# Attention and a gated FFN on one core: two head pairs in five bursts, pair nine turned on TensorE, and the first weight columns asked for earlier

## The chip, the cores and the metric

The kernel runs on one core of a Trainium2 chip. The metric is the device time of one execution in microseconds (us); lower is better. A core has TensorE (PE, matmuls, with its weight loads shown as PEld), VectorE (DVE), ScalarE (ACT), GpSimd (POOL) and SyncE (SP, which here only issues DMAs). SP, ACT and POOL issue the transfers that 16 DMA engines carry out.

## The reference, cut to what matters

Attention with 4 sink positions and a window of 128, on q, k and v of shape (4, 8, 768, 64), followed by a feed-forward layer with a ReLU gate on the 3072 tokens that result:

```python
scores = scale * np.matmul(q, k.transpose(0, 1, 3, 2))
keep = is_sink | in_window                 # rel >= 0 and rel < 128, or pos < 4
scores = np.where(keep, scores, -1000000000.0)
a = np.exp(scores - np.max(scores, axis=-1, keepdims=True))
a = a / (np.sum(a, axis=-1, keepdims=True) + 1e-09)
attn_out = np.matmul(a, v)
x = attn_out.transpose(0, 2, 1, 3).reshape(B * S, H * D)          # (3072, 512)
gate = np.maximum(x @ w_gate, 0.0)                                # w_gate (512, 1536)
out = (gate * (x @ w_val)) @ w_out                                # w_out (1536, 512)
```

Inputs and output are fp32; the matmuls run in bf16.

## The kernel before

The work is cut into 16 units, U[0] to U[15]: unit i is head pair i % 4 of batch i // 4. Pair nine is U[8], the first of batch 2. A unit passes through these steps:

- Loads (L105 to L120, issued on SP): k, q and v of the two heads go into one of four fp32 staging tiles. For a unit turned on PE (`xbar` false) k and q are read as contiguous rows of 1536 B; for one turned by DMA (`xbar` true, batches 2 and 3) in pieces of 256 B.
- Casts to bf16 (L122 to L130) on POOL; the first unit's k and q on DVE and ACT.
- Turning k and q so that the head dimension lies on the partitions: `T` (L140 to L156) is twelve PE transposes and two ACT copies, `X` (L132 to L136) is two DMA transposes on SP. `sinkk` (L158 to L162) then makes, on DVE, a copy of some key blocks with the four sink keys in front.
- `S(gi)` (L169 to L187), three groups: scores on PE for both heads at once (64 rows of the array each), the exponential on ACT, and a mask multiply on DVE. In batch 0 the mask is added on PE instead, by a matmul with `bias`.
- `V` and `norm` (L192 to L210, L268 to L280), two parts of 384 queries: on PE the sums (weights of ones) and the outputs (weights of v), each head in 64 columns of the array; on DVE a transpose, a reciprocal, a transpose and the multiply that writes xT, the FFN's input.

The FFN runs in 96 chunks (L285 to L298): 4 batches, 2 halves of 384 tokens and 12 blocks of 128 hidden columns. A chunk is four matmuls gp, a ReLU on ACT (gs), four matmuls vp, and on DVE the multiply hT = gs * vp. When a half is done, `ffn2` (L302 to L315) makes the output tiles, twelve matmuls op each, three of which are put behind each later chunk; ACT copies a finished tile and SP stores it.

The order is written out by hand and each engine keeps it. The attention work is a list of stages (L376 to L436): per unit [s(0), v, s(1), t, s(2), v0] for the first eight units, where v is part 1 of the unit before, t turns the next unit and v0 is part 0 of this one. For units 8 to 15 the six are joined to three: [v, s(0)], [t, s(1)], [v0, s(2)]. Stage t also issues the loads and casts of unit x+3, on SP and POOL, and the weights: each of four column quarters of w_gate and w_value is one DMA issued by POOL (L222 to L226), which converts to bf16 on the way. `PLAN` (L444) gives the number of stages that are to be emitted before chunk ci. In between, linearly:

```python
PLAN = ((0, 28), (24, 50), (48, 62), (71, 74))
```

So 28 stages (units 0 to 3 and the start of unit 4) run before chunk zero, and from chunk 24 on one stage comes every two chunks. I call what stands between two chunks a burst. PSUM pools: `ps_gv` (three buffers of one bank) holds gp and vp, and before chunk zero the sums and outputs of V and the transposes of k; `ps_at` (two buffers of two banks) holds scores and, from chunk zero on, the sums and outputs; `ps_op` (one) the op tile. The helper `held` (L343 to L347) sets a byte of the staging tile on DVE, so that the load behind it waits until DVE has come to that place.

Of the kernel before, what the change touches and what calls it, by code (L numbers as in the profile page):

```python
# [10 lines left out]
BF16 = mybir.dt.bfloat16  # L11
# [22 lines left out]
def kernel(  # L34
# [12 lines left out]
    nc = tc.nc  # L47
    B, H, S, D = q.shape
    assert (B, H, S, D) == (4, 8, 768, 64)
    NP = H // 2  # L50
    scale = 1.0 / (D ** 0.5)
    d_model, d_ff = moe_w_gate.shape
# [6 lines left out]
    xpool = ctx.enter_context(tc.tile_pool(name="xp", bufs=2))  # L59
# [18 lines left out]
    wg = const.tile([128, KO, d_ff], BF16, name="wg")  # L78
    wv = const.tile([128, KO, d_ff], BF16, name="wv")
# [10 lines left out]
    class Unit:  # L90
# [3 lines left out]
        def __init__(self, i):  # L94
            self.i, self.b, self.p, self.s = i, i // NP, i % NP, i % 2
            self.kn, self.qn, self.vn, self.stg = kn[i % 3], qn[i % 3], vn[i % 4], stg[i % 4]
            self.xbar = self.b>1
            self.biased = self.b == 0

        def staging(self, x):  # L100
# [118 lines left out]
            nc.tensor.matmul(out=warm_ps[0][:, 0:128], lhsT=ident[:], rhs=ident[:], start=True, stop=True,  # L219
                             skip_group_check=True)  # L220

    def load_w(c):  # L222
        n = d_ff // 4
        for w, dst in ((moe_w_gate, wg), (moe_w_val, wv)):
            nc.gpsimd.dma_start(out=dst[:, :, c * n:(c + 1) * n],  # L225
                                in_=w.rearrange("(ko ki) n -> ki ko n", ki=128)[:, :, c * n:(c + 1) * n])  # L226

    def load_wo(c):
        nc.gpsimd.dma_start(out=wo[:, 4 * c:4 * c + 4, :],
                            in_=moe_w_out.rearrange("(ko ki) n -> ki ko n", ki=128)[:, 4 * c:4 * c + 4, :])  # L230
# [12 lines left out]
    def setup_slot(s):  # L243
        nc.vector.memset(kT[s][:, S:872], 0.0)
# [20 lines left out]
    xTs = {}  # L265
    ready = {}

    def norm(u, part, pool=ps_at):  # L268

        c0, w, _ = PARTS[part]  # L270
        nb = w // 32
        o, sums = u.V(part, pool)
        r = rpool.tile([128, 2, 384], F32, name="R")
        rc = dpool.tile([128, 12], F32, name="rc")
        nc.vector.transpose(r[:, 0, 0:w], sums[:, 0:w])  # L275
        nc.vector.reciprocal(rc[:, 0:nb], r[:, 0, 0:w].rearrange("p (b j) -> p b j", j=32)[:, :, 0])
        a = rc[:, 0:nb]
        nc.vector.transpose(r[:, 1, 0:w], bass.AP(a.tensor, a.offset, [a.ap[0], [1, nb], [0, 32]]))  # L278
        ready[u.b, u.p] = c0 + w
        nc.vector.tensor_tensor(xTs[u.b][:, u.p, c0:c0 + w], o[:, 0:w], r[:, 1, 0:w], op=Alu.mult)  # L280
# [37 lines left out]
    with tc.manual_schedule():  # L318
        U = [Unit(i) for i in range(B * NP)]
        on_array = []  # L320

        def at(x):
            return U[x] if 0 <= x < len(U) else None

        def casts(u, what, eng=nc.gpsimd):
            for w in what:
                u.cast(w, eng)

        def load_t(b):

            nc.sync.dma_start(out=vt[b % 2][:], in_=v[b, :, 744:768, :].rearrange("h s d -> s h d"))  # L331

        def cast_t(b):
            nc.gpsimd.tensor_copy(v6[b % 2][0:24, :, :], vt[b % 2][:])

        def load(x):
            if not U[x].p:
                load_t(U[x].b)
            for f in (lambda e: U[x].load_kq("k", e), lambda e: U[x].load_kq("q", e),
                      lambda e: U[x].load_v(e, 0), lambda e: U[x].load_v(e, 1)):  # L340
                f(nc.sync)

        def held(x):  # L343

            if x < len(U):
                nc.vector.memset(U[x].stg[0:1, 0:1], 0.0)
                load(x)  # L347

        for y in ("k0", "q0", "k1", "q1", "v1", "t", "k2", "q2", "v2", "k3", "q3", "v3"):
            if y == "t":  # L350
                load_t(0)
            elif y[0] in "kq":
                U[int(y[1])].load_kq(y[0], nc.sync)
            else:
                for h in (0, 1) if y[0] == "v" else ("ab".index(y[0]),):
                    U[int(y[1])].load_v(nc.sync, h)
        nc.vector.memset(ones[:], 1.0)
        setup_pool()
        setup_m0()
        nc.scalar.activation(ee[0][:, 0, 0, 0:64], ones[:], Act.Exp, bias=0.0, scale=1.0)  # L360
        for h in range(2):
            U[0].load_v(nc.scalar, h)
        for x in range(2):
            nc.vector.memset(v6[x][:], 0.0)
        setup_slot(0)
        setup_slot(1)
        warm(36)
        casts(U[0], "k", nc.vector)
        casts(U[0], "q", nc.scalar)
        casts(U[1], "kq")  # L370
        casts(U[0], "v")
        cast_t(0)
        casts(U[1], "v")
        casts(U[2], "kqv")
        load(4)


        stages = []

        def unit_stages(x):  # L380
            u, prev, nxt = U[x], at(x - 1), at(x + 1)

            def s(gi):
                def f():
                    if gi == 0 and u.p == 0:
                        xTs[u.b] = xpool.tile([128, NP, S], BF16, name="xT")
                    if gi == 0 and nxt is not None and nxt.xbar:
                        nxt.X()
                    u.S(gi)
                    if x == 0 and gi < 2:  # L390
                        warm(5)
                return f

            def v():
                if prev is not None:
                    norm(prev, 1, ps_at if on_array else ps_gv)

            def t():
                if nxt is not None:
                    if not nxt.xbar:  # L400
                        nxt.T(not on_array)
                    nxt.sinkk()
                if x == 3:
                    load(6)
                elif x == 4:
                    load(7)
                elif x >= 5:
                    held(x + 3)
                if 4 <= x < 6:
                    for c in ((0,), (1, 2))[x - 4]:  # L410
                        load_wo(c)
                if at(x + 3) is not None:
                    casts(at(x + 3), "kqv")
                    if (x + 3) % NP == 0:
                        cast_t((x + 3) // NP)
                if x in (0, 1, 3, 4):
                    load_w((0, 1, 1, 2, 3)[x])
                if x == 0:
                    load(5)
            def v0():  # L420
                norm(u, 0, ps_at if on_array else ps_gv)

            def both(f, g):
                return lambda: (f(), g())
            if x < NP:
                return [s(0), v, s(1), t, s(2), v0]
            return [both(v, s(0)), both(t, s(1)), both(v0, s(2))] if x >= 8 else [s(0), v, s(1), t, s(2), v0]

        def first():
            U[0].T(True)  # L430
            U[0].sinkk()
            setup_m1()
        stages.append(first)
        for x in range(len(U)):
            stages += unit_stages(x)
        stages.append(lambda: norm(U[-1], 1))  # L436

        si = 0
        f2 = deque()
        total = len(stages)  # L440

        ORDER = [(0, h, m) for g in range(0, FM, 3) for h in range(2) for m in range(g, g + 3)]
        ORDER += [(b, h, m) for b in range(1, B) for h in range(2) for m in range(FM)]
        PLAN = ((0, 28), (24, 50), (48, 62), (71, 74))  # L444

        def want(ci):
            for (c0, w0), (c1, w1) in zip(PLAN, PLAN[1:]):
                if ci <= c1:
                    return w0 + (w1 - w0) * (ci - c0) // (c1 - c0)
            return total  # L450
        count = {}
        n = S // 2
        for ci, (b, h, m) in enumerate(ORDER):
            if b not in hTs:
                hTs[b] = hpool.tile([128, FM, S], BF16, name="hT", tag="hT")
            while si < min(total, want(ci)):
                stages[si]()
                si += 1
            if not ci:
                on_array.append(1)  # L460
            chunk(b, h * n, n, m)
            for _ in range(min(3, len(f2))):
                f2.popleft()()
            count[b, h] = count.get((b, h), 0) + 1
            if count[b, h] == FM:
                for t in range(3 * h, 3 * h + 3):
                    w = d_model // 2 if (b, t) == (B - 1, 5) else d_model
                    for c in range(0, d_model, w):
                        for mm in range(FM):
                            f2.append(lambda b=b, t=t, mm=mm, c=c, w=w: ffn2(b, t, mm, b == B - 1, c, w))  # L470
        while f2:
            f2.popleft()()
# [33 lines left out]
```

The softmax here doesn't subtract the row's maximum and nothing guards it: scores larger than these inputs give would overflow.

## Time and profile before

| what | value |
|---|---|
| median of 8 runs (lowest, highest) | 260.83 us (258.87, 262.15) |
| the profiled execution's own time | 262.15 us |
| its span in the profile | 260.3 us |
| PE busy | 248.5 us, 95% |
| DVE, ACT, POOL busy | 144.1, 115.8, 61.6 us |
| chunk matmuls gp and vp | 384 and 384, 78.5 and 78.1 us |
| output matmuls op | 70.6 us |
| mean granted PE clock | 0.998 |

Busy time of an engine counts instructions that overlap once. Matmuls overlap each other: the duration of one matmul is longer than its distance to the next, so PE work is read from the starts. A timeline line gives the start in the span, the time from the first start to the last end of the merged instructions, the engine, the line of code, the operation with what it writes and reads, how many there are, and in brackets the engine's idle time before it. A line of the waits gives who waited for whom, the total, how often, and the longest.

### The profile page before, as it was taken

The page shows a single profiled execution, that of the slowest core. Times are in us where ns is not written, and L with a number is a line of the kernel's source. Part 1 is how long each engine was busy: PE and PEld are TensorE (multiplying, and loading weights), DVE is VectorE, ACT ScalarE, POOL GpSimd, SP SyncE. Part 2 cuts the span into 40 slices and gives each one's busy share as a digit, 9 for nine tenths or more (in the row PEclk, how much of TensorE's full clock was granted, in tenths as well). Part 3 has the DMA queues.
Part 4 walks back from the last instruction along what each step waited for, and adds up shares of the span by engine and source line. Part 5 has one row for each costly group of instructions (what it writes and reads, how often), then busy time and mean ns, then how long its engine had stood idle before and what let it go on. Part 6 is the DMA issues. An engine that isn't in the chain of part 4 may idle for free.

```text
span 260.3 us, 5178 instructions
## 1 busy us (share of the span) xinstructions
PE 248.5 (95%) x2023; PEld 143.7 (55%) x2046; DVE 144.1 (55%) x313; ACT 115.8 (44%) x188; POOL 61.6 (24%) x94
## 2 busy tenths in 40 slices
PE   7899699999979999999999999999999999999994
PEld 7565355656545555555555555556555555555443
DVE  2498859786839574666666574756664322322100
ACT  2877753646524444354534444443533333333212
POOL 6679528901453320404030120000000000000000
PEclk9999999999999999999999999999999999999999
DMA  7999998999999956948792951311011001111132
GB/s 217 304 278 280 219 228 204 179 207 196 216 113 227 225 123 124 162 109 154 73 250 63 181 104 42 60 43 40 3 40 40 21 21 40 43 40 40 40 109 96
DMA packets 77320, 33.56 MB, mean 129 GB/s; under 512 B 64368, under 2 KB 74352, under 8 KB 77296
## 3 DMA queue, kind: packets, MB, share of 16 engines
q1 hardware_dynamic: 69920, 28.12, 48.6%
q0 software_dynamic: 5808, 4.72, 11.9%
q10 hardware_dynamic: 1568, 0.39, 0.7%
q8 instruction: 16, 0.26, 0.4%
q14 instruction: 8, 0.07, 0.1%
HBM read 28.51 MB, written 6.29 MB: 134 GB/s over the span
## 4 chain that ended last, share of the span: by engine, by line
PE 74%; DMA 12%; SPq 10%; POOL 1%; issue 1%; ACT 0%; DVE 0%; POOLq 0%; ACTq 0%; DVEq 0%
PE op L310 23%; PE gp L290 21%; PE vp L296 20%; PE ops L206 6%; DMA stg<-in_v_dram 6%; SPq L119 5%; DMA wv<-in_moe_w_val_dram 4%; PE sps L181 3%; SPq L114 2%; DMA kT<-kn 2%; SPq L111 1%; SPq L331 1%; POOL vn L129 1%; PE tkq L149 1%; POOL wg L225 0%
## 5 line engine op out<-in xcount | busy, mean ns | idle before, releaser
L298 DVE TENSOR_TENSOR hT<-gs,vp 128x384 bf16<-128x384 f32 x96 | 52.7, 550 | 55.5 <-PE vp L296 53.9
L290 PE MATMUL gp<-xT,wg 128*128 128x384 bf16 x384 | 78.5, 327 | 2.2 <-DVE hT L298 1.6
L296 PE MATMUL vp<-xT,wv 128*128 128x384 bf16 x384 | 78.1, 326 | 1.9 <-DMA wv<-in_moe_w_val_dram 1.9
L293 ACT ACTIVATE gs<-gp 128x384 f32<-128x384 f32 x96 | 47.1, 491 | 62.5 <-PE gp L290 61.3
L310 PE MATMUL op<-wo,hT 128*128 128x512 bf16 (+1 forms) x277 | 70.6, 370 | 1.2
L185 ACT ACTIVATE ee<-sps 128x1006 bf16<-128x1006 f32 (+2 forms) x48 | 46.1, 966 | 46.9 <-PE sps L181 46.8
L296 PEld LDWEIGHTS <-wv 128*128 128x128 bf16 x384 | 37.5, 98 | 27.0 <-DMA wv<-in_moe_w_val_dram 2.3
L290 PEld LDWEIGHTS <-wg 128*128 128x128 bf16 x384 | 34.0, 98 | 32.1 <-issue 6.1
L310 PEld LDWEIGHTS <-hT 128*128 128x128 bf16 x300 | 29.4, 98 | 25.0
L187 DVE TENSOR_TENSOR ee<-ee,msk 128x1006 bf16<-128x1006 bf16 (+2 forms) x36 | 25.1, 698 | 11.6 <-ACT ee L185 11.6
L126 POOL CAST kn<-stg 128x768 bf16<-128x768 f32 x15 | 13.1, 875 | 61.0 <-DMA stg<-in_k_dram 56.0
L314 ACT COPY ot<-op 128x512 f32<-128x512 f32 (+1 forms) x25 | 14.2, 569 | 24.5 <-PE op L310 22.5
L275 DVE STREAM_TRANSPOSE R<-ops 128x384 f32<-128x384 f32 x24 | 14.0, 582 | 12.7 <-PE ops L206 12.5
L278 DVE STREAM_TRANSPOSE R<-rc 128x384 f32<-128x384 f32 x32 | 18.5, 578 | 1.1
L280 DVE TENSOR_TENSOR xT<-ops,R 128x384 bf16<-128x384 f32 x32 | 17.8, 557 | 1.7
L206 PEld LDWEIGHTS <-ones 128*64 128x64 bf16 x288 | 12.3, 109 | 11.2 <-issue 10.8
L129 POOL CAST vn<-stg 128x768 bf16<-128x768 f32 x16 | 13.3, 830 | 14.8 <-PE gp L290 7.0
L126 POOL CAST qn<-stg 128x768 bf16<-128x768 f32 x15 | 13.0, 864 | 12.6 <-DMA stg<-in_q_dram 12.1
L206 PE MATMUL ops<-ee,vn 128*64 128x255 bf16 (+7 forms) x256 | 15.3, 240 | 0.2 <-DVE xT L280 0.2
L181 PE MATMUL sps<-qT,kT 64*128 64x251 bf16 (+2 forms) x128 | 14.7, 252 | 0.5 <-ACT qT L154 0.4
L181 PEld LDWEIGHTS <-kT 64*128 64x128 bf16 x128 | 6.3, 93 | 12.9 <-issue 10.9
L161 DVE COPY kTs<-kT 128x372 bf16<-128x372 bf16 x16 | 6.4, 399 | 11.0 <-ACT kT L154 6.9
(57 smaller groups left out, 141.1 us busy)
## 6 DMA issues: line engine op xcount, KB each, us to landing
stg<-in_k_dram SPq DMA_DIRECT2D x16, 384.0 KB, 4.7
stg<-in_q_dram SPq DMA_DIRECT2D x16, 384.0 KB, 5.3
out_dram<-ot SPq DMA_DIRECT2D x23, 256.0 KB, 2.0
stg<-in_v_dram SPq DMA_DIRECT2D x30, 192.0 KB, 5.3
wg<-in_moe_w_gate_dram POOLq DMA_DIRECT2D x4, 384.0 KB, 8.4
wv<-in_moe_w_val_dram POOLq DMA_DIRECT2D x4, 384.0 KB, 10.4
wo<-in_moe_w_out_dram POOLq DMA_DIRECT2D x3, 512.0 KB, 13.7
stg<-in_v_dram ACTq DMA_DIRECT2D x2, 192.0 KB, 7.7
```

The source lines that it names most:

```text
L126: cp((self.kn if what == "k" else self.qn)[:], self.staging(what).rearrange("p h (n d) -> p n h d", d=64))
L181: nc.tensor.matmul(out=ps[:, h, c:c + w], lhsT=self.kw(j, r), rhs=qT[s][r, qa:qa + w], start=not self.biased, stop=True, skip_group_check= ...
L185: nc.scalar.activation(x, ps[:, :, 0:c], Act.Exp, bias=0.0, scale=scale)
L187: nc.vector.tensor_tensor(x, x, bc(msk[:, m0:m0 + c], 2), op=Alu.mult)
L206: nc.tensor.matmul(out=ps[1 - what][64 * h:64 * h + 64, qa - q0:qa - q0 + w], lhsT=self.vw(j, h) if what else ones[:], rhs=ee[s][:, gi, h, ...
L278: nc.vector.transpose(r[:, 1, 0:w], bass.AP(a.tensor, a.offset, [a.ap[0], [1, nb], [0, 32]]))
L280: nc.vector.tensor_tensor(xTs[u.b][:, u.p, c0:c0 + w], o[:, 0:w], r[:, 1, 0:w], op=Alu.mult)
L290: nc.tensor.matmul(out=gp[:, 0:n], lhsT=wg[:, ko, m * 128:(m + 1) * 128], rhs=x[:, ko, c0:c0 + n], start=ko == 0, stop=ko == KO - 1)
L293: nc.scalar.activation(gs[:, 0:n], gp[:, 0:n], Act.Relu, bias=0.0, scale=1.0)
L296: nc.tensor.matmul(out=vp[:, 0:n], lhsT=wv[:, ko, m * 128:(m + 1) * 128], rhs=x[:, ko, c0:c0 + n], start=ko == 0, stop=ko == KO - 1)
L298: nc.vector.tensor_tensor(hT[:, m, c0:c0 + n], gs[:, 0:n], vp[:, 0:n], op=Alu.mult)
L310: nc.tensor.matmul(out=op, lhsT=hTs[b][:, m, t * 128:(t + 1) * 128], rhs=wo[:, m, c0:c0 + n], start=m == 0, stop=m == FM - 1)
```

## The change

Four things are edited.

1. `load_w` takes a range of 128-column thirds. The first 128 columns of the first quarter of w_gate and w_value are asked for on POOL between the casts of U[2]'s q and v, the other 256 between the casts of U[3]'s q and v. Before, the whole quarter was asked for behind U[3]'s casts.
2. `xbar` begins at unit 9 in place of unit 8: U[8] is turned on PE in stage t of U[7].
3. The first four units run s(0), s(1), v, t, s(2), v0.
4. From U[8] on two units u and w share five stages: scores (u,0) and (u,1); outputs of the unit before u, both parts (for U[7] part 1 alone), with the loads ahead and w's sink copy; scores (u,2) and (w,0); outputs of u, both parts; scores (w,1) and (w,2). The DMA transposes are issued with the first and third of them. There are 70 stages in place of 74, and `PLAN` has one more point.

The xT tile of a batch is allocated at its first use in `norm`, which adds no instruction. The diff, cut to its core:

```diff
-            self.xbar = self.b>1
+            self.xbar = i>8
...
-    def load_w(c):
-        n = d_ff // 4
-        for w, dst in ((moe_w_gate, wg), (moe_w_val, wv)):
-            nc.gpsimd.dma_start(out=dst[:, :, c * n:(c + 1) * n],
-                                in_=w.rearrange("(ko ki) n -> ki ko n", ki=128)[:, :, c * n:(c + 1) * n])
+    def load_w(c, which="gv", m=(0, 3)):
+        for x in which:
+            w, dst = (moe_w_gate, wg) if x == "g" else (moe_w_val, wv)
+            a, b = c * 384 + m[0] * 128, c * 384 + m[1] * 128
+            nc.gpsimd.dma_start(out=dst[:, :, a:b], in_=w.rearrange("(ko ki) n -> ki ko n", ki=128)[:, :, a:b])
...
-        casts(U[2], "kqv")
+        casts(U[2], "kq")
+        load_w(0, m=(0, 1))
+        casts(U[2], "v")
         load(4)
...
+        def ahead(x):
+            if x == 3:
+                load(6)
+            elif x == 4:
+                load(7)
+            elif x >= 5:
+                held(x + 3)
...
+            if x == 0:
+                casts(U[3], "k")
+                casts(U[3], "q")
+                load_w(0, "g", (1, 3))
+                load_w(0, "v", (1, 3))
+                casts(U[3], "v")
+            elif at(x + 3) is not None:
+                casts(at(x + 3), "kqv")
...
             if x < NP:
-                return [s(0), v, s(1), t, s(2), v0]
-            return [both(v, s(0)), both(t, s(1)), both(v0, s(2))] if x >= 8 else [s(0), v, s(1), t, s(2), v0]
+                return [s(0), s(1), v, t, s(2), v0]
+            return [s(0), v, s(1), t, s(2), v0]
+
+        def pair_stages(x):
+            u, w, nxt = U[x], U[x + 1], at(x + 2)
...
+            first_outs = outs(U[x - 1], 1) if x == 8 else outs(U[x - 1], 0, 1)
+            a = then(scores((u, 0), (u, 1)))
+            a_ = then(first_outs, lambda: ahead(x), w.sinkk)
+            c = then(scores((u, 2), (w, 0)))
+            d = then(outs(u, 0, 1), lambda: ahead(x + 1), lambda: nxt is not None and nxt.sinkk())
+            e = scores((w, 1), (w, 2))
+            first = [then(turn(w), a)] if w.xbar else [a, turn(w)]
+            second = [then(c, turn(nxt))] if nxt is None or nxt.xbar else [c, turn(nxt)]
+            return first + [a_] + second + [d, e]
...
-        for x in range(len(U)):
+        for x in range(8):
             stages += unit_stages(x)
-        stages.append(lambda: norm(U[-1], 1))
+        for x in range(8, len(U), 2):
+            stages += pair_stages(x)
+        stages.append(lambda: (norm(U[-1], 0), norm(U[-1], 1)))
...
-        PLAN = ((0, 28), (24, 50), (48, 62), (71, 74))
+        PLAN = ((0, 28), (6, 32), (24, 50), (48, 62), (71, 70))
```

## The prediction, as recorded before the run

> **What bounds the kernel now.** I first read the busy table in 40 slices, then the list of waits, then the timelines of TensorE (PE) and VectorE (DVE) around each PE gap. The slices show PE full except at the start, around slices 5 (33 us) and 11 (75 us), and at the end:
>
> ```profile
> PE   7899699999979999999999999999999999999994
> DMA  7999998999999956948792951311011001111132
> ```
>
> The span is 260.3 us, its execution took 262.15 us, the median is 260.83. So time can come only from the two holes or from PE work. The list of waits names the holes:
>
> ```profile
> DVE kTs L161 <- DMA kT<-kn: 4.1, 1, 4.1
> ...
> PE vp L296 <- DMA wv<-in_moe_w_val_dram: 1.9, 1, 1.9
> PE gp L290 <- DVE hT L298: 1.6, 1, 1.6
> ...
> PE gp L290 <- DMA wg<-in_moe_w_gate_dram: 0.6, 1, 0.6
> ```
>
> The first hole is 0.59 + 1.91 = 2.50 us: chunk zero waits for the first weights (issued at 21.62 and 22.49, landed 8.8 and 10.6 us later). The second is 1.58 us: DVE stands 4.06 us before the sink copy of pair nine (U[8]), whose kT comes from a DMA transpose issued late, and an hT multiply queued behind it holds a PSUM buffer that gp needs.
>
> What DVE did under the first hole matters too (start, duration):
>
> ```profile
> 29.17 0.56 DVE L280 TENSOR_TENSOR xT<-ops,R 128x384 bf16<-128x384 f32 x1
> 29.66 0.69 DVE L187 TENSOR_TENSOR ee<-ee,msk 128x1006 bf16<-128x1006 bf16 x1
> 30.27 0.58 DVE L275 STREAM_TRANSPOSE R<-sums 128x384 f32<-128x384 f32 x1
> ...
> 31.82 0.56 DVE L280 TENSOR_TENSOR xT<-ops,R 128x384 bf16<-128x384 f32 x1
> ```
>
> The xT that chunk zero reads is ready at 29.73; the next normalization ends at 32.38. It reads PSUM from the pool that gp and vp share.
>
> In the full stretch the bursts of attention between chunks are the only thing on PE that is not a dense stream:
>
> ```profile
> 93.46 0.81 PE L310 MATMUL op<-wo,hT 128*128 128x512 bf16 x3
> 94.20 0.53 PE L206 MATMUL ops<-ee,ones 128*64 128x119 bf16 x10
> 94.58 0.50 PE L206 MATMUL ops<-ee,vn 128*64 128x119 bf16 x8
> 94.92 0.18 PE L206 MATMUL ops<-ee,v 128*64 128x20 bf16 x2
> 95.03 0.28 PE L181 MATMUL sps<-qT,kT 64*128 64x255 bf16 x2
> 95.15 0.27 PE L181 MATMUL sps<-qT,kTs 64*128 64x248 bf16 x2
> 95.35 0.82 PE L290 MATMUL gp<-xT,wg 128*128 128x384 bf16 x4
> ...
> 98.82 0.59 PE L310 MATMUL op<-wo,hT 128*128 128x512 bf16 x2
> 99.35 0.28 PE L181 MATMUL sps<-qT,kT 64*128 64x251 bf16 x2
> 99.47 0.27 PE L181 MATMUL sps<-qT,kTs 64*128 64x248 bf16 x2
> 99.67 0.82 PE L290 MATMUL gp<-xT,wg 128*128 128x384 bf16 x4
> ```
>
> Read the starts. Three op matmuls take 0.65 (86.51 to 87.16, where gp follows); before a V they take 0.74, so entering V costs 0.09. Two take 0.43 (82.40 to 82.83), before an S 0.53: entering S costs 0.10. Inside V the sums take 0.38 and the equal columns of ops 0.45 until S starts: leaving V costs 0.07 (0.05 for the shorter part, 89.20, 89.53, 89.91). The first pair of S takes 0.12, the equal second one 0.20 until gp: leaving S costs 0.08.
>
> [...] V runs as 128*64, S as 64*128, the chunks as 128*128[...], and S to S or V to V would not switch. [...] with the weights in flight the v load issued at 28.95 took 12.0 us, those before 22 us mostly 5.3 to 7. [...] Pair nine's k and q come in 256 B pieces now; its q took 18.7 us, beside weights, so size and company aren't separated.
>
> **The change, part by part.**
>
> (1) Early first columns. POOL finishes the casts of U[2]'s k and q at 15.36 and then stands until 16.83 for v. The two new issues (0.75 each, as the other weight issues) fit there: free. The other two thirds go out at about 19.9, before U[3]'s v cast, which moves from 20.28 to about 21.5; its reader, V at 26.8, has 4 us left. The four issues replace two, and later POOL work stands where it stood. If the 8.8 to 10.6 us to landing hold, the first columns are there by 27 and the rest by 31.3: chunk zero no longer waits. What is late next is DVE. With E the end of the xT multiply (29.73), gp0 starts at E + 0.05; vp0 needs the buffer that the first transpose of the next normalization frees, E + 0.6 (mask) + 0.6; gp1 follows at E + 1.9; vp1 needs the end of that normalization (E + 2.65); the transposes of U[5] take 0.67 (46.59 to 47.26). So gp2 starts at E + 4.0. Before it was at 35.79 = E + 6.06. Gain 2.06, not 2.5. Cover: if the first columns come after 29.7, each us late costs one.
>
> (2) Scores one and two ahead of V in the first four pairs. Moving one S (0.85) before V gives DVE the kT copy earlier: its two waits of 0.47 and 0.50 for ACT's kT copy go, but DVE then waits about 0.3 twice for the later sums. Walking PE, ACT and DVE by these durations puts E 0.4 earlier. Against it stands the queue sharing: 0.5 MB of weights now travels while k and q of U[3] and U[4] do (q of U[3] landed 18.95, its cast ended 19.93, PE wanted it at 20.8). Bounds: gain 0.5 to loss 1.5. I take a gain of 0.2.
>
> (3) Pair nine on PE. Twelve transposes add 0.67 on PE; the two ACT copies (0.80 each) have room (ACT is busy 4 to 5 of 10 us there). SP loses two transposes and loads k and q in 1536 B runs. The 1.58 goes, with 0.1 before the S at 80.55. Net gain 1.0. Bounds: 1.68 is the most; a loss of 0.67 if the wait only moves to pair ten, the first on the DMA transpose now.
>
> (4) Five bursts for six. Before, two pairs made twice [V,S] [S] [V,S]: 4 x 0.09 + 4 x 0.06 + 2 x 0.10 + 6 x 0.08 = 1.28. After: [S,S] [V,V] [S,S] [V,V] [S,S]: 2 x 0.09 + 2 x 0.06 + 3 x (0.10 + 0.08) = 0.84. Saves 0.44, times four: 1.8. Bounds: 0.3 a group of two pairs less if S,S and V,V pay as apart (0.3 in all), 2.4 if every one of the six switches is worth 0.10. What [V,V] puts at risk: two normalizations (2.03 each), the staging memset and the sink copy (0.45) now stand ahead of hT on DVE. From the burst's start: V done 0.8, norms done 4.8, sink copy done 5.2. The next burst, whose second S reads kTs, is two chunks later at 1.55 + 3.9 = 5.45 and gets there at 5.75: 0.55 of slack. PSUM for vp two chunks on is wanted at 6.65, hT is done at 5.75. DMA transposes: issued a burst earlier, about 4 us to landing (80.93 to DVE's use at 84.97), used after some 8.7.
>
> (5) The new plan holds one stage back in the first chunks and is level at chunk 24. Weights must then come earlier: wv quarter three landed at 51.65, wanted at 55.69 - 2.3 - 0.7 = 52.7. Free with 1 us left. Allocating xT later costs nothing: no instruction.
>
> Sum: 2.06 + 0.2 + 1.0 + 1.8 = 5.1. On the execution of 262.15: 257.05. The median is 0.5% below that execution, so 5.1 x 0.995 = 5.0 off 260.83: **255.8**.
>
> **The rivals.** A: queue sharing. Loads of U[3] and U[4] land 1.5 later, PE waits at their transposes, (2) becomes a loss: 5.1 - 1.7 = 3.4, 257.4. For it: 12.0 against 5.3 us landing. Against: POOL waited for v, not for k and q, at 16 us. B: the DMA stall moves to pair ten: 3.5 left, 257.3. For: it is the next on that path, in small pieces. Against: its transposes at 80.93 caused no wait and pair nine's loads ahead of it now get lighter. C: merged bursts save nothing beyond 0.3: 257.2. D, slower: at each of the seven [V,V] bursts with a sink copy, DVE is late and holds PE. It decides from 5.1 / 7 = 0.73 of stall each, so with the sink copy ending at 6.5 instead of 5.2; at the 1.58 that pair nine's cost, 11.1 - 5.1 = 6 slower, 266.8. For: 1.58 shows that a late sink copy reaches PE. Against: DVE is busy 6 of 10 us there.
>
> **How the numbers follow.** 255.8 (its own range 254.6 to 256.9) has 0.58, A 0.13, B 0.09, C 0.07, D 0.07, more than I count (2.5 for (1), 2.4 for (4): 254.3) 0.06. Low 254.0 and high 258.5 leave out D and tails. A measurement of this kernel can tell about 0.5% (1.3 us) from no change: faster by more has A to C and most of the rest, 0.87; same 0.05; slower 0.08.
>
> **What would show it.** Right: no wait of vp for wv; a DVE-made gap of some 0.7 us near 30; no DVE wait for kT near 75; [S,S] in 0.52 with 0.10 ahead; PE's dense stretch without gaps. Wrong: PE waits for casts at 20 to 26 (A), a kTs wait near 80 (B), gp waiting for hT after [V,V] (D).

## The result, and the profile after

The changed kernel takes 256.32 us in the median of 11 runs (255.37 to 256.97); the kernel before took 261.21 us beside it (32 runs, 258.87 to 263.37). The ratio is 0.9826, with a 95% interval of 0.98 to 0.9852; executions over 1.5% above the fastest of their kernel are left out of a ratio, so it is not the quotient of the medians. The prediction was 255.8 us. The profiled execution took 256.04 us and has a span of 254.2 us; before it was 262.15 and 260.3, and as that execution lay 0.94 above the median of its kernel, the two profiles differ by more (6.1 us) than the medians do (4.9 us).

The busy table of the changed kernel in 40 slices. Against before, the 7 in the twelfth slice of the PE row has become a 9 and the 6 in the fifth an 8:

```profile
PE   7999899999999999999999999999999999999994
DMA  7999999999995889679929513111001100111132
```

PE is busy 97% of the span, before 95%. The list of waits has none of the four lines that were shown of before (kTs for kT, vp for wv, gp for hT, gp for wg). What PE still waits for at the start is DVE. The timeline of PE from gp of chunk zero on, before and after:

```profile
30.43 0.82 PE L290 MATMUL gp<-xT,wg 128*128 128x384 bf16 x4 [0.59 <-DMA wg<-in_moe_w_gate_dram]
33.16 0.82 PE L296 MATMUL vp<-xT,wv 128*128 128x384 bf16 x4 [1.91 <-DMA wv<-in_moe_w_val_dram]
...
35.79 0.81 PE L290 MATMUL gp<-xT,wg 128*128 128x384 bf16 x4
```

```profile
29.24 0.81 PE L293 MATMUL gp<-xT,wg 128*128 128x384 bf16 x4 [0.59 <-DVE xT L283]
30.37 0.81 PE L299 MATMUL vp<-xT,wv 128*128 128x384 bf16 x4 [0.32 <-DVE R L278]
31.01 0.81 PE L293 MATMUL gp<-xT,wg 128*128 128x384 bf16 x4
...
33.22 0.81 PE L293 MATMUL gp<-xT,wg 128*128 128x384 bf16 x4
```

E, the end of the xT multiply, is now 29.18 (28.62 + 0.56). So vp0 starts at E + 1.19, gp1 at E + 1.83 and gp2 at E + 4.04; the prediction had E + 1.2, E + 1.9 and E + 4.0. The first columns were asked for at 15.08 and 15.95 and landed 5.8 us later each.

The bursts of the dense stretch, first [S,S] and then [V,V], each with the gp that follows:

```profile
76.08 0.28 PE L181 MATMUL sps<-qT,kT 64*128 64x255 bf16 x2
76.20 0.27 PE L181 MATMUL sps<-qT,kTs 64*128 64x248 bf16 x2
76.31 0.27 PE L181 MATMUL sps<-qT,kT 64*128 64x251 bf16 x2
76.41 0.27 PE L181 MATMUL sps<-qT,kTs 64*128 64x248 bf16 x2
76.62 0.82 PE L293 MATMUL gp<-xT,wg 128*128 128x384 bf16 x4
...
89.96 0.47 PE L206 MATMUL ops<-ee,ones 128*64 128x255 bf16 x8
90.29 0.45 PE L206 MATMUL ops<-ee,vn 128*64 128x255 bf16 x8
90.60 0.52 PE L206 MATMUL ops<-ee,ones 128*64 128x119 bf16 x10
90.96 0.50 PE L206 MATMUL ops<-ee,vn 128*64 128x119 bf16 x8
91.29 0.18 PE L206 MATMUL ops<-ee,v 128*64 128x20 bf16 x2
91.41 0.82 PE L293 MATMUL gp<-xT,wg 128*128 128x384 bf16 x4
```

Read the starts. Inside [S,S] one group follows the other at the distance of one pair of matmuls (0.10 to 0.12), and only the last pair takes 0.21 until gp. The burst takes 0.54, where its two groups took 0.32 each when they stood alone; [V,V] takes 1.45, where its parts took 0.71 and 0.83.

Where the time came from is read from the starts of gp, chunk by chunk, after against before. At chunk 2 it is 2.57 earlier (0.38 of it because this whole execution began earlier: its first scores start at 7.88, before at 8.26). At chunk 20 it is 2.57 again; between the two, the new plan moves it by up to 0.9. At chunk 21 it is 1.90 earlier (0.67 for the twelve transposes of pair nine), and at chunk 23 it is 3.56 earlier, as pair nine's hole is gone. Of before and after, the gp behind that hole:

```profile
77.58 0.81 PE L290 MATMUL gp<-xT,wg 128*128 128x384 bf16 x4 [1.58 <-DVE hT L298]
```

```profile
74.03 0.82 PE L293 MATMUL gp<-xT,wg 128*128 128x384 bf16 x4
```

From there the lead swings between 2.8 and 4.5 up to chunk 55, as the bursts stand at other chunks than before, and reaches 6.29 at chunk 71; at the end it is 6.1.

### The profile page after: what moved, and what is told of

Its sections match the earlier page's. It is cut to its first block, busy times and chain, and to the rows that moved or that the text cites. A ratio compares the mean times of both kernels' runs of the same rounds, so it can differ in the third digit from the quotient of the medians.

```text
span 254.2 us, 5212 instructions
## 1 busy us (share of the span) xinstructions
PE 246.4 (97%) x2036; PEld 144.6 (57%) x2058; DVE 146.6 (58%) x313; ACT 117.2 (46%) x190; POOL 64.5 (25%) x96
## 3 DMA queue, kind: packets, MB, share of 16 engines
HBM read 28.51 MB, written 6.29 MB: 137 GB/s over the span
## 4 chain that ended last, share of the span: by engine, by line
PE 90%; DVE 4%; DMA 2%; ACT 1%; issue 1%; SPq 0%; DVEq 0%; ACTq 0%
PE gp L293 26%; PE vp L299 24%; PE op L313 24%; PE ops L206 7%; PE sps L181 5%; DMA stg<-in_q_dram 2%; PE sps L176 1%; PE tkq L149 1%; DVE R L281 1%; DVE xT L283 1%; DVE R L278 1%; DVE kTs L161 1%; PE sums L206 1%; PE tq L149 0%; ACT ee L185 0%
## 5 line engine op out<-in xcount | busy, mean ns | idle before, releaser
L301 DVE TENSOR_TENSOR hT<-gs,vp 128x384 bf16<-128x384 f32 x96 | 52.0, 549 | 50.5 <-PE vp L299 47.5
L185 ACT ACTIVATE ee<-sps 128x1006 bf16<-128x1006 f32 (+2 forms) x48 | 44.6, 962 | 16.2 <-PE sps L181 15.9
L187 DVE TENSOR_TENSOR ee<-ee,msk 128x1006 bf16<-128x1006 bf16 (+2 forms) x36 | 26.7, 741 | 18.6 <-ACT ee L185 18.3
L129 POOL CAST vn<-stg 128x768 bf16<-128x768 f32 x16 | 14.2, 889 | 17.3 <-DMA stg<-in_v_dram 12.7
L181 PE MATMUL sps<-qT,kT 64*128 64x251 bf16 (+2 forms) x128 | 13.6, 250 | 0.0
L181 PE MATMUL sps<-qT,kTs 64*128 64x248 bf16 (+1 forms) x96 | 11.7, 253 | 0.2 <-DVE kTs L162 0.2
```

The costliest lines, as they stand in the source:

```text
L181: nc.tensor.matmul(out=ps[:, h, c:c + w], lhsT=self.kw(j, r), rhs=qT[s][r, qa:qa + w], start=not self.biased, stop=True, skip_group_check= ...
L185: nc.scalar.activation(x, ps[:, :, 0:c], Act.Exp, bias=0.0, scale=scale)
L187: nc.vector.tensor_tensor(x, x, bc(msk[:, m0:m0 + c], 2), op=Alu.mult)
L301: nc.vector.tensor_tensor(hT[:, m, c0:c0 + n], gs[:, 0:n], vp[:, 0:n], op=Alu.mult)
```

## The experiments

The twelve ran in four groups, and the kernel before beside each; its median was 261.07 to 261.37 us. "Over after" means against 256.32 us. A ratio has an interval of 0.2 to 0.6% to each side, so differences of the medians under some 1.3 us are read together with the profile.

### Four parts, undone one by one

The first columns asked for as before:

```diff
-        load_w(0, m=(0, 1))
...
-                casts(U[3], "k")
-                casts(U[3], "q")
-                load_w(0, "g", (1, 3))
-                load_w(0, "v", (1, 3))
-                casts(U[3], "v")
+                casts(U[3], "kqv")
...
-            if x in (1, 3, 4):
+            if x in (0, 1, 3, 4):
```

> The changed kernel with the weights asked for as before: the whole first quarter behind the casts of pair four. My theory (part 1 of the sum): the wait of vp for wv comes back at chunk zero, gp of chunk two returns from 33.2 to about 35.4 us, and the time rises by 2.1 to 2.5 us to about 258.6. Rival: the new order of the first four pairs, not the early columns, made the gain, and the weights land early enough anyway: at most 0.5 us, about 256.7.

Measured: 258.75 us (256.49 to 261.82), ratio 0.9873 (0.9815 to 0.9931). The median is where the theory had it, 2.4 over after, but not for the reason that it gave alone: the spread is 5.3 us, against 1.6 of after. The profiled execution was the fastest of them: there wv landed at 31.03, where in the profile of before it landed at 33.12, vp waited 0.83 us, and gp of chunk two came at 33.71, not at the expected 35.4. What makes the others so much slower is taken up below (e12).

Pair nine turned by DMA again:

```diff
-            self.xbar = i>8
+            self.xbar = self.b>1
```

> The changed kernel with pair nine turned by DMA transposes again. My theory (part 3): the hole of 1.6 us near 75 us returns and 0.67 us of PE transposes goes: slower by 1.0, about 257.3. Rival: the hole came from loads that lay behind later weights; everything before it now runs 2.6 us earlier while the loads do not, so the hole grows by that and the kernel is slower by 2.5 to 3.5, 259 to 260. Second rival: the hole doesn't come back, and the kernel is faster by 0.7, 255.6.

Measured: 257.23 us (256.26 to 258.9), ratio 0.9852 (0.9807 to 0.9897), 0.9 over after; its profiled execution took 257.62. The timelines of DVE and of PE in that kernel show the hole again:

```profile
74.25 0.29 DVE L161 COPY kTs<-kT 128x372 bf16<-128x372 bf16 x1 [3.31 <-DMA kT<-kn]
```

```profile
75.13 0.81 PE L293 MATMUL gp<-xT,wg 128*128 128x384 bf16 x4 [1.32 <-DVE hT L301]
...
78.06 0.28 PE L181 MATMUL sps<-qT,kT 64*128 64x251 bf16 x2 [0.50 <-DVE xT L283]
```

By the starts of gp, the hole and the wait behind it cost 2.13 from chunk 21 to chunk 24, and the missing transposes give 0.67 back: 1.46 in this execution. The prediction said 1.0. This run also separates what the prediction could not: with the same weights in company, q of pair nine took 17.1 us in pieces of 256 B (asked for at 48.21, landed at 65.33) and 8.5 us in runs of 1536 B in the changed kernel (47.91 and 56.41). The size of the pieces is what made it slow, by 8.6 us here.

The first four units in their old order, [s(0), v, s(1), t, s(2), v0]:

```diff
-            if x < NP:
-                return [s(0), s(1), v, t, s(2), v0]
             return [s(0), v, s(1), t, s(2), v0]
```

> The changed kernel with the first four pairs in their old order (scores, outputs, scores). My theory (part 2): xT of chunk zero comes 0.2 to 0.5 us later, slower by that, about 256.6. Rival: the order is worth nothing because loads set the pace there: no difference, 256.3. Second rival: earlier weights starve pair three and four in the old order, 1 us or more slower, 257.3.

Measured: 256.96 us (256.63 to 257.98), ratio 0.9844 (0.98 to 0.9887), 0.6 over after, which is less than these runs can tell from nothing. In its profile gp of chunk two is 0.49 later than in the changed kernel, but the order is not what made it so. DVE in the changed kernel, and then in e3:

```profile
28.62 0.56 DVE L283 TENSOR_TENSOR xT<-ops,R 128x384 bf16<-128x384 f32 x1
29.10 0.73 DVE L187 TENSOR_TENSOR ee<-ee,msk 128x1006 bf16<-128x1006 bf16 x1
```

```profile
28.62 0.56 DVE L283 TENSOR_TENSOR xT<-ops,R 128x384 bf16<-128x384 f32 x1
29.18 1.15 DVE L187 TENSOR_TENSOR ee<-ee,msk 128x1006 bf16<-128x1006 bf16 x1
```

The xT that chunk zero reads is ready at 29.18 in both; the mask multiply behind it took longer. It took 0.85 to 1.32 us in the profiles of e2, e4, e5, e6 and e10 too, which begin just as the changed kernel does, and their gp of chunk two is 0.04 to 0.43 later. Counted from the first scores, xT is ready 0.24 later in e3 (21.54 against 21.30 us), the size that was forecast, but in those five it comes after 21.20 to 21.75. So what this part is worth stays open.

The last eight units in their old three stages each, with the old end of the plan:

```diff
+            if x >= 8:
+                return [lambda: (v(), s(0)()), lambda: (t(), s(1)()), lambda: (v0(), s(2)())]
...
-        for x in range(8):
+        for x in range(len(U)):
             stages += unit_stages(x)
-        for x in range(8, len(U), 2):
-            stages += pair_stages(x)
-        stages.append(lambda: (norm(U[-1], 0), norm(U[-1], 1)))
+        stages.append(lambda: norm(U[-1], 1))
...
-        PLAN = ((0, 28), (6, 32), (24, 50), (48, 62), (71, 70))
+        PLAN = ((0, 28), (6, 32), (24, 50), (48, 62), (71, 74))
```

> The changed kernel with the last eight pairs in their old stages, six bursts for two pairs, and 74 stages. By the recorded sum (part 4) it is slower by 1.8, 258.1. By the burst durations of the two profiles, 20.6 against 22.9 us with their entries, it is slower by 2.3, 258.6. Rival: only the entries of the four bursts count, 4 x 0.2 = 0.8, 257.1, and the rest of the gain near the end has another cause.

Measured: 258.92 us (258.43 to 259.36), ratio 0.9908 (0.9877 to 0.9939), 2.6 over after. By the chunks: 0.30 later than after up to chunk 23, 2.93 later from chunk 72 on, so 2.63 lie between, where the bursts are. That is above the predicted 1.8.

### Is it the change of mode?

The price of a change of the array's mode was only inferred from starts. Two kernels put it to the test: a one-column matmul between the two groups of each [S,S] (12 places) and the two parts of each [V,V] (7 places), in the whole-array mode or in the mode that the array is already in. Its result is overwritten by the next matmul.

```diff
+            if second:
+                nc.tensor.matmul(out=ps[:, 0, 0:1], lhsT=ident[:], rhs=ident[:, 0:1], start=True, stop=True, skip_group_check=True)
...
+                if second:
+                    nc.tensor.matmul(out=ps[1][:, 0:1], lhsT=ident[:], rhs=ident[:, 0:1], start=True, stop=True, skip_group_check=True)
```

In the control the two are `lhsT=ident[0:64, :], rhs=ident[0:64, 0:1]` and `out=ps[1][0:64, 0:1], lhsT=ident[:, 0:64]`.

> The changed kernel with one tiny matmul of the whole 128x128 array (one column) put between the two groups of scores of each merged burst (12 places) and between the two parts of the outputs (7 places). It is written into a place that the next matmul overwrites, so the output is unaffected; it only adds two changes of the array's mode at each place. Theory (the merged bursts gain by the changes of mode that they leave out, about 0.095 us each): 19 x (2 x 0.095 + 0.03 for the matmul itself) = 4.2 us over the changed kernel, about 260.5. Rival (the merged bursts gain by something else, fewer semaphore waits or fewer gaps between chunks): only the matmuls themselves, at most 0.8, 257.1 or less, and the same as the control e6.

> Control for e5: the same 19 one-column matmuls in the mode that the array is already in (64 rows between the scores, 64 columns between the outputs). Theory: 19 x 0.02 to 0.04 = 0.4 to 0.8 us over the changed kernel, 256.7 to 257.1, and no longer steps of 0.2 in the bursts. Rival: the same as e5, if an instruction more costs as much as a change of mode.

Measured: e5 260.13 us (ratio 0.9965, 0.9944 to 0.9986), e6 257.14 us (0.9854, 0.9811 to 0.9898): 3.8 and 0.8 over after. The same burst in the timeline of e5:

```profile
76.29 0.28 PE L183 MATMUL sps<-qT,kT 64*128 64x255 bf16 x2
76.41 0.27 PE L183 MATMUL sps<-qT,kTs 64*128 64x248 bf16 x2
76.61 0.18 PE L173 MATMUL sps<-ident 128*128 128x1 bf16 x1
76.72 0.28 PE L183 MATMUL sps<-qT,kT 64*128 64x251 bf16 x2
```

The second pair now takes 0.20 until the whole-array matmul, and that one, a single column, 0.11 until the next S; in e6 it starts 0.10 after the pair and S follows 0.01 later:

```profile
76.90 0.27 PE L183 MATMUL sps<-qT,kTs 64*128 64x248 bf16 x2
77.00 0.17 PE L173 MATMUL sps<-ident 64*128 64x1 bf16 x1
77.01 0.29 PE L183 MATMUL sps<-qT,kT 64*128 64x251 bf16 x2
```

By the starts of the chunks, e5 loses 3.98 us in the 19 places beyond what it had lost before them, e6 0.46: 0.209 and 0.024 a place. The places between scores and those between outputs cost alike (0.20 to 0.22 each in e5, 0.02 to 0.03 in e6). The difference, 0.185, is two changes, so one change of mode costs 0.093 us. The rival, that something else than the changes of mode made the gain, falls for all but the 0.4 us that (4) below leaves open.

The loads of the weights (PEld) suggest what the 0.093 us are. Of the one column in e5, and then in e6:

```profile
76.61 0.10 PEld L173 LDWEIGHTS <-ident 128*128 128x128 bf16 x1 [0.21 <-DVE xT L287]
```

```profile
76.94 0.09 PEld L173 LDWEIGHTS <-ident 64*128 64x128 bf16 x1
```

In the same mode, the load starts 0.03 to 0.10 us ahead of its matmul at the twelve places between scores, and so runs beside the one before. Behind a change of mode it starts with its matmul, at most 0.005 us ahead, at all 80 changes of e5 from U[8] on and at all 42 of the changed kernel. It takes 0.09 to 0.11 us (0.097 in the mean), and 0.09 in e6 with half the weights. So a change costs about what one load costs that nothing hides; that this is its cause is not shown.

### Further along the same way

Can the first normalization of U[4]'s stretch be had earlier, ahead of U[4]'s mask?

```diff
+            if x == NP:
+                return [v, s(0), s(1), t, s(2), v0]
```

> The changed kernel with part 1 of the outputs of U[3] ahead of the first scores of U[4], so that VectorE does that normalization before U[4]'s mask multiply. Theory (after the weights came early the start of the chunks is bound by VectorE, E + mask + normalization): vp of chunk zero at E + 0.7 in place of E + 1.2, gp of chunk two at E + 3.4 in place of E + 4.0, 0.6 less, about 255.7. Rival (the weights or the scores still set the start): no gain, 256.3.

Measured: 257.11 us (255.89 to 257.26), ratio 0.9844 (0.9801 to 0.9887). No gain. The profile shows what took the wait's place: vp0 now follows gp0 at once (29.77 after 29.12), as expected, but gp1 waits 0.56 for the multiply that ends the normalization, which frees a PSUM buffer of the pool that they share. gp of chunk two starts at 33.11, 0.11 earlier than in the changed kernel, which is within what executions of one beginning differ by (33.22 to 33.65, see e3). The theory had overlooked which of the buffers comes third.

U[4] to U[7] joined in pairs too:

```diff
...
-        for x in range(8):
+        for x in range(NP):
             stages += unit_stages(x)
-        for x in range(8, len(U), 2):
+        for x in range(NP, len(U), 2):
             stages += pair_stages(x)
...
+        PLAN = ((0, 27), (2, 29), (24, 42), (48, 53), (71, 61))
```

The first pair of these begins with part 1 of U[3]'s outputs; U[7]'s outputs come both in the third pair's first [V,V].

> e7's order, and U[4] to U[7] also joined in pairs (two bursts of scores and two of outputs in place of twelve bursts per pair; 61 stages). By the price of a change of mode: per pair of units three bursts of scores (0.2 each) and two of outputs (0.18 each) less, 0.96, twice 1.9; with e7's 0.5 about 253.9. Rival: VectorE, with two normalizations, mask multiplies and the sink copy in a row, gets late with hT in this denser stretch and gives it back: 256 or more, with waits of gp for hT in the profile.

Measured: 261.06 us (259.15 to 261.46), ratio 0.9984 (0.9954 to 1.0015), 4.7 over after. The rival's time, though the waits are others than it named: the second S of a burst finds its PSUM buffer still held. Two such waits:

```profile
48.28 0.28 PE L181 MATMUL sps<-qT,kT 64*128 64x251 bf16 x2 [1.10 <-ACT ee L185]
...
62.02 0.28 PE L181 MATMUL sps<-qT,kT 64*128 64x255 bf16 x2 [0.75 <-DVE stg L349]
```

Here a burst of scores stands one chunk of 1.3 us (at 48.28) or two (at 62.02) behind a burst of outputs, whose two normalizations take DVE 4 us and hold the two buffers of `ps_at`. At 62.02 S starts as the second of them ends (61.96); at 48.28 it comes when the exponential of the first S is done, which suggests that it takes over that one's buffer. The same with the stages set by hand, two chunks behind each [V,V]:

```diff
...
+        PLAN = ((24, 43), (48, 54), (71, 62))
+        AT = (1, 2, 3, 4, 5, 6, 8, 10, 11, 12, 14, 15, 16, 18, 20, 22)
...
+            if ci < 24:
+                return 27 + sum(c <= ci for c in AT)
```

> e8 again (U[4] to U[7] in pairs) with its stages put by hand: two chunks between a burst of outputs and the next of scores, the first normalization before chunk zero in the chunk pool, the first two groups of scores apart. Theory (e8's stalls, 0.7 to 1.2 us each, came from bursts one chunk apart, so that the normalizations still held the scores' PSUM buffers): the stalls go and the six changes of mode saved per pair show, 1.9 in all, about 254.4. Rival (VectorE and ScalarE have no room in this stretch whatever the spacing): 256.3 or more, with waits for ee, stg or hT left.

Measured: 257.77 us (257.58 to 258.12), ratio 0.9901 (0.9864 to 0.9937), 3.3 less than e8 and 1.4 over after. Three stalls are left, of 0.73, 0.76 and 0.73 us, all of S for DVE two chunks behind a [V,V]. They are as long as those that e8 had at that distance (0.75 and 0.72); what went are others, the one at 48.28 among them. Two chunks without op matmuls are 2.6 us, and from chunk 24 on, with three op each, 3.9, where no such stall is seen: the merged burst needs more than the former. Theory and rival each hold in part. Whether three chunks behind each [V,V] would fit into the first 24 was not tried. No version here beats the changed kernel.

How near the changed kernel itself is to such a stall (rival D of the prediction) was asked with two idle transposes on DVE behind the normalizations of seven [V,V]:

```diff
+                    if len(parts) == 2:
+                        if y.i == 8:
+                            nc.vector.memset(pad[0][:], 0.0)
+                        for _ in range(2):
+                            nc.vector.transpose(pad[1][:], pad[0][:])
```

> The changed kernel with two idle transposes of 128x384 on VectorE (1.2 us) behind the normalizations of seven merged bursts of outputs, ahead of the sink copy. They read and write spare tiles; the output is unaffected. By the recorded margin (sink copy at 5.2, wanted at 5.75, slack 0.55): 7 x 0.65 = 4.6 us over the changed kernel, 260.9. By the trace of the changed kernel (hT done 0.4 before gp of two chunks later wants its PSUM buffer): 7 x 0.8 = 5.6, 261.9. Rival (VectorE has much more room, as it is busy 57% of the time): no change, 256.3.

Measured: 260.54 us in the median (259.2 to 261.03, and one execution of 318.4), ratio 0.9982 (0.9962 to 1.0001), 4.2 over after; 0.6 of that arose before the first [V,V]. The waits that came are of the kind that D had described, a chunk matmul for hT and S for the sink copy:

```profile
97.81 0.81 PE L299 MATMUL vp<-xT,wv 128*128 128x384 bf16 x4 [0.49 <-DVE hT L301]
111.96 0.28 PE L181 MATMUL sps<-qT,kTs 64*128 64x248 bf16 x2 [0.36 <-DVE kTs L162]
```

3.65 us in seven places are 0.52 each in the mean (0.12 to 0.69), for 1.2 us of ballast: the slack is about 0.7, from 0.5 to 1.1. The prediction had 0.55.

### The first columns alone, and the clock

Does the early columns' gain need the other edits? The kernel before, with the first edit alone:

```diff
...
-        casts(U[2], "kqv")
+        casts(U[2], "kq")
+        load_w(0, m=(0, 1))
+        casts(U[2], "v")
...
+                if x == 0:
+                    casts(U[3], "k")
+                    casts(U[3], "q")
+                    load_w(0, "g", (1, 3))
+                    load_w(0, "v", (1, 3))
+                    casts(U[3], "v")
...
```

> The kernel before with the early first columns alone (the first edit of the change, nothing else). Theory: the wait for weights goes and VectorE bounds the start, 2.06 us less on the profiled execution, about 259.1 median, and a smaller spread of times than before (some 1.5 us in place of 4.5), since what varied is when the weights land. Rival (the columns only help with the other edits): 261.

Measured: 259.69 us (258.35 to 262.63), ratio 0.9969 (0.9935 to 1.0003), 1.4 below before. In its profile gp of chunk two starts at 33.70, 2.09 earlier than in the profile of before; the prediction had 2.06. But the gain of the medians is smaller, its interval just reaches no change, and the expected spread of 1.5 us was not seen (4.3, though all but two of its 14 executions lie within 2.5).

The times of before fall into groups by the granted clock. In the 107 executions of before in the four groups of runs, 61 have a mean clock of 0.998 or more and a median of 260.65 us; 46 have 0.986 to 0.993 and a median of 261.75. Of e1's six executions three have 0.987 to 0.992 (259.84 to 261.82); its other three took 256.49 to 257.67. Of the 12 executions of the changed kernel none is below 0.998, of the 97 of e2 to e10, which have the early columns too, two are below 0.997 (0.992, and 0.757 in the one of 318.4 us), and of the 14 of e11 two (0.993). A last run put the columns still later, so that the wait had to be long:

```diff
-        load_w(0, m=(0, 1))
...
-                casts(U[3], "k")
-                casts(U[3], "q")
-                load_w(0, "g", (1, 3))
-                load_w(0, "v", (1, 3))
-                casts(U[3], "v")
+                casts(U[3], "kqv")
+            elif x == 1:
+                casts(U[4], "kq")
+                load_w(0)
+                casts(U[4], "v")
```

> The changed kernel with the whole first quarter of w_gate and w_value asked for behind the casts of U[4]'s k and q, some 10 us later than the first columns are now. What it is for: the spread of the times. In the kernel before, 5 to 18 of 13 to 36 executions show a mean granted clock of 0.986 to 0.993, and these take 1 to 3 us longer; with the early columns hardly any do. Theory (a wait of PE near 30 us that is long enough makes the array's clock fall to half [...]): gp of chunk zero at about 34, vp at 36, so 4 to 5 us of wait; nearly every execution at a mean clock of 0.993 or less; the matmuls behind the wait take twice as long in the trace; in all 6 to 7 us over the changed kernel, about 263. Rival (the clock falls for a cause outside the kernel, and only the landing of the weights differs): clock 1.0 in most executions, 4 to 5 us more, about 261.

Measured: 262.68 us (261.06 to 264.05), ratio 1.006 (1.0037 to 1.0084), 6.4 over after, within the 6 to 7 of the theory. All 19 executions have a mean clock of 0.993 or less: 0.993 (4), 0.986 or 0.987 (11), 0.98 (4). The rival falls. Its profile, PE behind the wait:

```profile
33.57 1.46 PE L293 MATMUL gp<-xT,wg 128*128 128x384 bf16 x4 [4.86 <-DMA wg<-in_moe_w_gate_dram]
36.22 1.46 PE L299 MATMUL vp<-xT,wv 128*128 128x384 bf16 x4 [1.19 <-DMA wv<-in_moe_w_val_dram]
37.48 1.49 PE L293 MATMUL gp<-xT,wg 128*128 128x384 bf16 x4
...
41.23 0.81 PE L293 MATMUL gp<-xT,wg 128*128 128x384 bf16 x4
```

and its table by stretches of 4 us, where PEclk is the column behind POOL's:

```profile
24.00:28.00 4.00, 3.52 (x68) 2.64 (x64) 3.73 (x10) 3.43 (x5) 3.44 (x5) 1.00 0.95 234
28.00:32.00 4.00, 0.71 (x18) 0.37 (x10) 3.72 (x7) 1.68 (x2) 4.00 (x7) 0.86 1.21 261
32.00:36.00 4.00, 1.46 (x4) 0.43 (x4) 1.19 (x2) 0.49 (x1) 3.09 (x4) 0.50 1.24 205
36.00:40.00 4.00, 3.78 (x12) 1.79 (x13) 0.56 (x1) 0.49 (x1) 0.00 (x0) 0.50 1.27 191
40.00:44.00 4.00, 4.00 (x34) 2.79 (x33) 1.92 (x4) 2.53 (x5) 1.86 (x3) 0.86 1.15 317
```

The clock is half for 0.28 x 4 + 4 + 4 + 0.28 x 4 = 10.2 us, four matmuls take 1.46 in place of 0.81, and at 41.2 they are back at 0.81. The mean clocks of the 19 executions lie in three steps. If the clock was at half in all of them, as the trace shows for this one, the means give an estimate of the time at half speed: 2 x 0.007 x 260 = 3.6 us for 0.993, 6.8 for 0.987 and 10.4 for 0.98, the last near the 10.2 read here. So 15 of the 19 lost more than the least step. What the expected 6 to 7 us held beyond the wait, some 2 us, was an estimate too; a mean clock of 0.993 over 260 us is 1.8. The fall is at 30.9, if it is a single one (half clock for the last 28% of the stretch up to 32), 2.2 us behind the end of the last matmul at 28.7. What length of wait a fall needs is not shown. That an execution of before with 0.993 has its fall near 30 us is inferred, as no profile of before happened on one; what is shown is that making that wait long brings a mean clock of 0.993 or less to every execution, and that with the early columns, where it is short, that is rare: in none of the 12 executions of the changed kernel.

## Why the prediction was right, point by point

**(1) First columns, 2.06.** Right in its mechanism and, on the profiled execution, in its size: vp0, gp1 and gp2 came within 0.07 of the places named, and the columns alone moved gp2 by 2.09. That it came so near is partly luck: this profile has the shortest mask multiply and the earliest gp2 of the six that begin alike (33.22 to 33.65 us). On the medians the gain is less: executions with a full clock gain 1.2 to 1.3 (260.66 to 259.48 from before to e11; 257.64 to 256.32 from e1, with three such executions, to after). So the 2.50 us of waiting in the profile of before was probably more than usual, which a single profile can't tell. In its place comes something that the working didn't have: 46 of 107 executions of before also lost clock.

**(2) First order, 0.2.** Not decided: e3's 0.6 is within the noise, and its profile has xT ready at the same time. Of the two expected waits of 0.3 for sums only one of 0.18 came. What rival A had named came at U[5]: its k and q landed at 28.34 and 30.18, 3.2 and 4.0 us later than before; from issue to landing they took 9.0 and 8.0 us, before 5.5 and 5.3. It cost nothing that shows, as PE didn't want them then.

**(3) Pair nine, 1.0.** Right: 1.66 for the hole and the wait behind it, less 0.67 for the transposes, 1.0 by the chunks; e2 gives 0.9 by the medians and 1.46 by its profile. No wait for kT came at pair ten (rival B).

**(4) Five bursts for six, 1.8.** The right mechanism and a term that was too small: 2.6 in e4. The mis-sized term is the cost of leaving a mode, put at 0.08 after S and 0.05 to 0.07 after V by comparing starts. By e5 and e6 entering and leaving are 0.185 together, for scores and outputs alike, so leaving costs about 0.09, as much as entering. The merged stages have 24 changes fewer (66 to 42 from U[8] on): 24 x 0.093 = 2.2, near the 2.4 that the prediction gave as the upper bound. Of the 2.6, 0.4 isn't accounted for. Sixteen changes straight from V to S fell away with the rest, a kind that e5 doesn't price. Rival C (0.3) falls.

**(5) Plan.** Free, as said: wv's third quarter landed at 48.24, with no wait for it.

**D, the slower case.** It didn't happen, and its working was sound: the slack is about 0.7 us where 0.55 was worked out, and ballast on DVE brought just its waits. e8 shows what it costs where the bursts stand closer.

**The sum.** 255.8 was predicted and 256.32 measured. The undone parts sum to 2.4 + 0.9 + 0.6 + 2.6 = 6.5 over after, more than the 4.9 that the whole brings; with the full clock's 1.3 for the first it is 5.4. Part of the nearness is thus that (1) was too large for the median and (4) too small. How much of the rest is overlap of the parts and how much the uncertainty of some 1 us of each run stays open. Two sums of its cases are off by a little: 0.44 more for (1) and 0.6 more for (4) lead from 255.8 to 254.8, not to 254.3, and rival B's 1.67 lead to 257.5, not to 257.3.

## What to carry to other kernels

Where small matmuls in a tiled mode stand between dense ones, count the changes of mode: each cost 0.093 us here, so joining bursts of one mode pays (2.6 us by e4) as long as the engine that empties their PSUM has room until the next burst (e8, where it had not, took 4.7 over after), which has to be worked out in time and not in busy shares (0.7 us were left on a DVE that was idle 42% of the span). And a wait of PE early in a kernel of some us is to be priced twice, once for itself and once for the clock that it may take away: with 2.50 us of waiting in the profile of before, 46 of 107 executions lost clock, with 6.05 in that of e12 all 19. A single profile may show neither at its usual size.

## What the runs showed of the hardware that was not expected

- A single column in another mode costs about as much as a whole group of scores inside a burst (0.23, from 76.08 to 76.31): 0.209 us for one 128x1 matmul of the whole array between two groups of S or two parts of V, 0.024 in their own mode. The load of the first weights in the new mode starts with its matmul (at most 0.005 us ahead, at 80 changes of e5 and 42 of the changed kernel), and one load takes 0.097 us in the mean, near the 0.093 of one change.
- With the columns as late as in e12 (a wait of 4.86 us in its profile) every one of 19 executions lost clock. In the profiled one it was half for 10.2 us; the fall came about 2.2 us after the last matmul and outlasted the wait. Chunk two came 8.0 us later than in the changed kernel, some 3 of which are slow matmuls and transposes: the four groups and the transposes ahead of it took 6.5 us, where 4 x 0.65 + 0.67 = 3.3 is their time at full clock.
- The same q load, beside the same weights, took 17.1 us in 256 B pieces (e2) and 8.5 us in 1536 B runs (the changed kernel).
- One and the same mask multiply on DVE took 0.73 to 1.32 us in the six profiles that begin alike (the changed kernel, e2, e4, e5, e6 and e10). Why is open.
